# Half-unit staging of q and k, a re-woven gMLP tail, and a last unit by batch, in an attention + gMLP kernel

**Chip, cores, metric.** One core of one Trainium2 chip. The metric is device time in microseconds (us) of one execution. Each run has a state, fast or slow; ratios and comparisons here use fast runs.

## The reference

Linear attention with an exponential feature map, then a gated MLP over all heads of a position (cut to what matters):

```python
# q, k, v: (8 batches, 8 heads, 576, 64); w_phi: (64, 128)
def phi(x):
    proj = einsum('bhsd,df->bhsf', x, w_phi)
    proj = proj - max(abs(proj), axis=-1, keepdims=True)
    return concatenate([exp(proj), exp(-proj)], axis=-1)
q_p, k_p = phi(q), phi(k)
kv = einsum('bhsf,bhsd->bhfd', k_p, v); z = sum(k_p, axis=2)
x = einsum('bhsf,bhfd->bhsd', q_p, kv) / (einsum('bhsf,bhf->bhs', q_p, z) + 1e-6)   # heads joined: (8, 576, 512)
u, v = split(gelu_tanh(x @ w_in), 2)                    # w_in: (512, 1024)
v_n = (v - mean(v)) / sqrt(var(v) + 1e-6) * g_ln
out = x + (u * (w_sg @ v_n + b_sg)) @ w_out             # w_sg: (576, 576)
```

## The kernel before

The eight batches are four *units* of two batches, and a unit's attention is two *halves* of four heads. A half passes through: load of q and k (cast to 16 bit by GpSimd's DMAs, into `qks`), two merges on VectorE (`qk`), four DMA transposes (`qkT`), `nat` (projections, maxima, exponentials of k, v scaled on GpSimd), `kvsum`, `projnum`. After both halves comes the *win stage* (product with w_in, GELU, statistics, normalisation), and the *tail* (gate and output product) is woven into the two attention *stretches* of the next unit. The parts that the change touches, cuts marked `# ...`:

```python
qks = stage.tile([128, 2, H, NS, D], FP16, ...)      # a whole unit: 8 heads; the pool has one buffer
def merge(qks, h2):                                   # VectorE, into the single buffer qk
    ...
def prep(qks, h2):
    qk = merge(qks, h2)
    # ... four nc.sync.dma_start_transpose(qkT <- qk)

def norm(res):
    # ... Newton steps for 1/sqrt
    for n in range(NS):
        for pl, dst in parts:
            nc.vector.tensor_scalar(out=dst[pl, :], in0=vts[n][pl, :], ...)
            nc.gpsimd.tensor_tensor(out=dst[pl, :], in0=dst[pl, :], in1=g_bc[pl, :], op=ALU.mult)

for u in range(NU):
    if more:                                          # q and k of the next unit, all 16 loads at once
        nqk = new_qk()
        load(nc.gpsimd, u + 1, q, nqk[:, 0], both)
        load(nc.gpsimd, u + 1, k, nqk[:, 1], both)
        nT0 = prep(nqk, 0)
    # stretch 1: nat of half 1, projnum of half 0, 14 turns of the old unit's tail
    # stretch 2: nat of the next half 0, kvsum and projnum of half 1, the rest of the tail
    # ... prep(nqk, 1), win stage
weave((behind, 30, 0, 1))                             # last unit's tail
```

Program order is a wish: a scheduler orders each engine's queue by expected readiness. Line numbers in profiles belong to each kernel's own text; L91, L103 and L106 are the same merge in different kernels.

## Time and profile before

| | before |
|---|---|
| median of 3 runs | 403.94 us (402.97 to 407.26) |
| span of the profiled run, mean granted TensorE clock | 399.4 us, 0.885 |
| first bn_stats of units 0, 1, 2, 3, and end | 122.4, 200.0, 281.4, 350.6, 399.4 us |

The first bn_stats (VectorE's statistics of the v half) marks the start of a unit's win stage. The distances between these marks show which part of the kernel a gain lies in. The prediction below shows and reads the lines of the page.

### The profile page before, as it was taken

The page shows a single profiled execution, that of the slowest core. Times are in us where ns is not written, and L with a number is a line of the kernel's source. Part 1 is how long each engine was busy: PE and PEld are TensorE (multiplying, and loading weights), DVE is VectorE, ACT ScalarE, POOL GpSimd, SP SyncE. Part 2 cuts the span into 40 slices and gives each one's busy share as a digit, 9 for nine tenths or more (in the row PEclk, how much of TensorE's full clock was granted, in tenths as well). Part 3 has the DMA queues.
Part 4 walks back from the last instruction along what each step waited for, and adds up shares of the span by engine and source line. Part 5 has one row for each costly group of instructions (what it writes and reads, how often), then busy time and mean ns, then how long its engine had stood idle before and what let it go on. Part 6 is the DMA issues. An engine that isn't in the chain of part 4 may idle for free. (4 is left out here: it accounts for less than half of the span.)

```text
span 399.4 us, 7803 instructions
## 1 busy us (share of the span) xinstructions
PE 286.6 (72%) x3021; PEld 193.5 (48%) x3021; DVE 285.7 (72%) x633; ACT 245.8 (62%) x521; POOL 168.9 (42%) x189
## 2 busy tenths in 40 slices
PE   0532622866519978697898587978997879997794
PEld 0422511654405656574455465745565655544562
DVE  4549924898437999977599999756898971589530
ACT  1446113979904769478977494689767945974022
POOL 7547700567900554658208346062174550007300
PEclk9975565698858989999999699899998999999699
DMA  8988998209988200069990510544900002300015
GB/s 142 209 184 115 153 241 138 52 5 186 169 121 190 50 2 0 2 156 256 212 214 2 93 29 2 174 118 127 182 2 1 2 3 107 126 7 1 2 53 184
DMA packets 64708, 40.01 MB, mean 100 GB/s; under 512 B 35872, under 2 KB 61344, under 8 KB 64672
## 3 DMA queue, kind: packets, MB, share of 16 engines
q1 hardware_dynamic: 46128, 27.65, 29.5%
q0 software_dynamic: 18544, 11.88, 21.1%
q8 instruction: 23, 0.38, 0.4%
q14 instruction: 13, 0.11, 0.1%
HBM read 33.55 MB, written 9.44 MB: 108 GB/s over the span
## 5 line engine op out<-in xcount | busy, mean ns | idle before, releaser
L258 POOL TENSOR_TENSOR vx<-vs,vx 128x1024 f16<-128x1024 f32 (+2 forms) x48 | 71.2, 1500 | 98.8 <-ACT vx L249 89.2
L242 ACT ACTIVATE kp<-psk 128x512 f16<-128x512 f32 x144 | 81.1, 642 | 43.1 <-DVE MK L236 43.0
L316 ACT ACTIVATE qp<-pp 128x512 f16<-128x512 f32 x128 | 73.1, 657 | 10.9 <-PE pp L311 10.8
L410 POOL TENSOR_TENSOR vt<-vt,g_bc 128x512 f16<-128x512 f16 x32 | 37.7, 1207 | 80.5 <-DVE vt L408 80.2
L236 DVE TENSOR_REDUCE MK<-psk 128x4 f32<-128x512 f32 x72 | 49.1, 682 | 13.6 <-PE psk L233 13.0
L421 PE MATMUL pw<-WsgT,vt 128*128 128x288 f16 x256 | 49.6, 311 | 11.3 <-DVE uT L425 10.2
L238 DVE TENSOR_REDUCE MQ<-psq 128x4 f32<-128x512 f32 x72 | 48.9, 679 | 0.3 <-PE psq L235 0.2
L235 PE MATMUL psq<-wq,qkT 128*128 128x128 f16 x288 | 32.3, 239 | 16.9 <-DVE MQ L238 14.2
L442 ACT ACTIVATE osb<-po 128x512 f32<-128x512 f32 x36 | 22.0, 641 | 33.7 <-PE po L438 31.7
L233 PE MATMUL psk<-wk,qkT 128*128 128x128 f16 x288 | 31.8, 238 | 13.8 <-ACT qkT L217 12.2
L425 DVE TENSOR_TENSOR uT<-pw,uT 128x288 f16<-128x288 f32 x64 | 28.5, 447 | 15.9 <-PE pw L423 10.1
L421 PEld LDWEIGHTS <-vt 128*128 128x128 f16 x256 | 25.8, 105 | 25.2 <-issue 14.8
L335 PE MATMUL pn<-kvz,qp 128*128 128x65 f16 x512 | 28.5, 203 | 11.4 <-ACT qp L316 10.1
L335 PEld LDWEIGHTS <-qp 128*128 128x128 f16 x512 | 23.0, 103 | 27.5 <-ACT qp L316 23.6
L369 PE MATMUL pv<-Win,xT 128*128 128x512 f16 x144 | 35.9, 386 | 0.5 <-ACT vt L372 0.5
L382 PE MATMUL pu<-xT,Win 128*128 128x384 f16 x192 | 35.2, 325 | 0.2
L372 ACT ACTIVATE vt<-pv 128x512 f16<-128x512 f32 x36 | 21.1, 596 | 22.2 <-PE pv L369 21.9
L91 DVE COPY qk<-qks 128x2304 f16<-128x2304 f16 x16 | 13.7, 879 | 27.7 <-DMA qkT<-qk 11.8
L311 PE MATMUL pp<-qkT,wqm 66*128 66x512 f16 x72 | 29.2, 419 | 5.8 <-DMA qkT<-mT 3.3
L233 PEld LDWEIGHTS <-qkT 128*128 128x128 f16 x288 | 22.2, 107 | 20.2 <-ACT qkT L217 13.5
L235 PEld LDWEIGHTS <-qkT 128*128 128x128 f16 x288 | 22.7, 108 | 18.7 <-issue 17.8
L408 DVE TENSOR_SCALAR vt<-vt,agg,y 128x512 f16<-128x512 f16 x32 | 31.1, 1034 | 0.4
(92 smaller groups left out, 552.5 us busy)
## 6 DMA issues: line engine op xcount, KB each, us to landing
out_dram<-osb SPq DMA_DIRECT2D x32, 256.0 KB, 2.3
vs<-in_v_dram SPq DMA_DIRECT2D x16, 320.0 KB, 3.8
vs<-in_v_dram SPq DMA_DIRECT2D x16, 256.0 KB, 4.6
qks<-in_q_dram POOLq DMA_DIRECT2D x6, 320.0 KB, 10.1
qks<-in_k_dram POOLq DMA_DIRECT2D x6, 320.0 KB, 16.4
qks<-in_q_dram POOLq DMA_DIRECT2D x6, 256.0 KB, 9.0
qks<-in_k_dram POOLq DMA_DIRECT2D x6, 256.0 KB, 16.0
Win<-in_moe_w_in_dram POOLq DMA_DIRECT2D x1, 1024.0 KB, 12.7
```

Of the source, the lines that this page charges most:

```text
L233: nc.tensor.matmul(psk[:, i, :], qkT[:, n, i, :], wk[:], start=True, stop=True)
L235: nc.tensor.matmul(psq[:, i, :], qkT[:, n, i, :], wq[:], start=True, stop=True)
L236: nc.vector.tensor_reduce(out=MK[:, n, :], in_=psk[:], axis=AX.X, op=ALU.max, apply_absolute_value=True)
L238: nc.vector.tensor_reduce(out=MQ[:, n, :], in_=psq[:], axis=AX.X, op=ALU.max, apply_absolute_value=True)
L242: nc.scalar.activation(out=kp[:, e], in_=psk[:], func=AF.Exp, scale=(1.0, -1.0)[e])
L258: nc.gpsimd.tensor_tensor(out=vx[e][:, :, x0:x0 + nn, 0:64], in0=vs[:, :, n0:n1, :], in1=vx[e][:, :, x0:x0 + nn, 64:65].broadcast_to([128, ...
L316: nc.scalar.activation(out=qp[:, e], in_=pp[:], func=AF.Exp, scale=(1.0, -1.0)[e])
L335: nc.tensor.matmul(pn[:, i, :], lhs, rhs, start=(x == 0), stop=(x == len(terms) - 1))
L369: nc.tensor.matmul(pv[:], xT[:, c, n * 128:n * 128 + 128], Win[:, c, DF2:DFF], start=(c == 0), stop=(c == 3))
L382: nc.tensor.matmul(pu[:], Win[:, c, d * 128:d * 128 + 128], xT[:, c, 384 * g:384 * g + 384], start=(c == 0), stop=(c == 3))
L410: nc.gpsimd.tensor_tensor(out=dst[pl, :], in0=dst[pl, :], in1=g_bc[pl, :], op=ALU.mult)
L421: nc.tensor.matmul(pw[:], vts[5 * i + m][:, dd], WsgT[:, m, c0:c0 + 288], start=(m == 0), stop=False)
```

## The change

The intent: halve each q/k load, so that the start needs less data before it can go on, and issue a load only behind the transposes of the half before, so that the two don't cross; take g off GpSimd; spread the tail more evenly; let the last unit's gate of one batch begin before the other batch is normalised. Core of the diff:

```diff
-        return stage.tile([128, 2, H, NS, D], FP16, tag="qks", name="qks")
+    def load_qk(k, res, behind=None):
+        qks = stage.tile([128, 2, HH, NS, D], FP16, tag="qks", name="qks")   # half a unit
+        for t, src in enumerate((q, k_)):
+            for ins in load(nc.gpsimd, k // 2, src, qks[:, t], ...):
+                if behind is not None:
+                    tc.add_manual_dep(ins.ins, behind.ins.name, sync, reason="loads behind the transposes")
+                yield
-                nc.gpsimd.tensor_tensor(out=dst[pl, :], in0=dst[pl, :], in1=g_bc[pl, :], op=ALU.mult)
+                nc.vector.tensor_tensor(out=dst[pl, :], in0=dst[pl, :], in1=g_bc[pl, :], op=ALU.mult)
     def back(res):                                   # the tail
         yield from gate(res, 0)
-        # gate(res, 1) woven with wout of slots 0 to 3
+        yield from wout(res, range(0, 4))
+        yield from gate(res, 1)
         yield from wout(res, range(4, 9))
+        for k in range(NK):                          # over halves
+            qT[k + 2], last = prep(qks.pop(k + 2))
+            w.append((load_qk(k + 3, qks, last), 9, LD0, LD1))        # woven in between 0.3 and 0.8
+            # ... nat(k + 1), projnum(k)
+            w.append((behind, (12, 14)[h2], 0, 1))
+            # ... last unit:
+                weave((win_v(res, range(NS)), 10, 0, 1))
+                weave((norm(res, 0, 5, (0, 1)), 7, 0, 0.5), (win_u(res, [(0, 288), (288, 288)]), 9, 0, 1))
+                weave((gate(res, 0), 9, 0, 1), (norm(res, 5, 9, ()), 6, 0, 0.5))
+                # ... the other half of win_u, wout, gate(1), wout
```

Also: the query maxima's high and low parts (`hl`) are split from PSUM after the transpose, no longer in on-chip memory before it; w_in, g and w_out load later, and the bias row with w_sg earlier.

## The prediction

> **What bounds the kernel now.** I read the page first. No engine is full over the span, so I looked for where each stands still.
>
> ```profile
> PE 286.6 (72%) x3021; PEld 193.5 (48%) x3021; DVE 285.7 (72%) x633; ACT 245.8 (62%) x521; POOL 168.9 (42%) x189
> ...
> PEclk9975565698858989999999699899998999999699
> DMA  8988998209988200069990510544900002300015
> ```
>
> PE and DVE are equal at 72%; in the first 12 slices the DMA row is nearly full and PE's clock is low. So the kernel is two things: a start that lives on transfers, and a steady part in which PE, DVE and ACT take turns. Next I cut the span by stage in the windows view (columns: window, length, busy time of PE, PEld, DVE, ACT, POOL, PE's clock, DMA share, GB/s):
>
> ```profile
> 52.00:65.30 13.30, 2.84 (x22) 1.92 (x23) 1.53 (x3) 1.08 (x2) 0.00 (x0) 0.50 1.12 202
> ...
> 105.00:117.00 12.00, 0.71 (x10) 0.30 (x8) 0.32 (x1) 5.02 (x10) 4.61 (x5) 0.71 1.29 160
> ...
> 276.00:302.00 26.00, 23.09 (x215) 13.63 (x213) 22.44 (x50) 19.66 (x38) 12.45 (x11) 1.00 0.42 100
> ```
>
> Two windows, 25 us together, hold almost no work on any engine while the transfers are saturated. The DVE timeline names the waits in its brackets:
>
> ```profile
> 27.91 1.61 DVE L170 CAST b<-bs 128x576 f16<-128x576 f32 x1 [5.15 <-DMA bs<-in_moe_b_sg_dram]
> ...
> 38.63 4.23 DVE L276 CAST hl<-MQ 128x36 f16<-128x36 f32 x1
> ...
> 57.36 0.76 DVE L91 COPY qk<-qks 128x2304 f16<-128x2304 f16 x1 [5.34 <-DMA vs<-in_v_dram]
> 64.55 0.76 DVE L91 COPY qk<-qks 128x2304 f16<-128x2304 f16 x1 [6.44 <-DMA qks<-in_k_dram]
> ...
> 116.69 0.76 DVE L91 COPY qk<-qks 128x2304 f16<-128x2304 f16 x1 [11.76 <-DMA qkT<-qk]
> ```
>
> DVE works in order, so a merge (L91) that waits for a load holds every reduction queued behind it. Up to 65 us it waits for the whole next unit's q and k, at 105 to 117 for four DMA transposes that must empty the one qk buffer. Last, the normalisation before the gate, by its source line:
>
> ```profile
> L408 DVE TENSOR_SCALAR vt<-vt,agg,y x32: 407/1236/1303, 133.6 to 370.0; 128x512 f16<-128x512 f16 x32
> L408 DVE TENSOR_SCALAR vm<-vt,agg,y x8: 1128/1184/1234, 136.5 to 365.3; 64x512 f16<-64x512 f16 x8
> ```
>
> The triple is minimum, median and maximum in ns. An operation of 407 ns usually takes 1236, because GpSimd multiplies the preceding slot by g (L410, 1207 ns each) at the same time. In the last unit PE pays for it, as its timeline shows:
>
> ```profile
> 366.34 0.30 PE L421 MATMUL pw<-WsgT,vt 128*128 128x288 f16 x1 [0.61 <-POOL vt L410]
> 367.50 0.30 PE L423 MATMUL pw<-wsgm,vm 128*128 128x288 f16 x1 [0.86 <-POOL vm L410]
> ...
> 371.61 1.12 PE L421 MATMUL pw<-WsgT,vt 128*128 128x288 f16 x4 [3.21 <-DVE uT L425]
> ```
>
> **What the Trainium skill says.** (1) SBUF — State Buffer, section Who interferes with whom: GpSimd and a DVE instruction in a 2-port mode share a port pair, and whoever issues second blocks until the first is done; tensor_scalar can be such an instruction. The trace agrees: 407 against 1236 ns. The hl cast (L276) has a median of 169 ns and takes 4232 ns once, at 38.6 us, while GpSimd works. (2) VectorE: DVE Perf Modes, section The perf-mode tier table: a 16-bit tensor_tensor reaches 2x, 1224 ns at 2048 elements, hence an estimate of (256+151)/0.96 = 424 ns at 512. No such operation runs on DVE before, so the trace cannot say. (3) DMA: Bandwidth & Descriptors, section Issuing engines are not separate DMA queues: all queues share the 16 DMA engines. The trace agrees: a transpose lands after 3.4 us at best and 14.4 at worst, the worst beside a q/k load. (4) TensorE: Matmul & The Clock Gate, section What's actually happening: an idle PE falls to half clock. The 0.50 in the window above agrees.
>
> **The change part by part.** From the order view of both kernels as built.
>
> *Staging by half unit.* The bytes stay the same. Each load is now half as large, and is issued only when the transposes of the half before have landed. Before the second half's reductions can start, DVE now needs three halves of q and k rather than four. One half is 8 loads of 128 to 160 KB on the way in, 2.36 MB of float32 (4 heads x 2 batches x 576 x 64 x 4 bytes x 2 tensors). Unit 1's 4.7 MB plus v's 1.2 MB took from 42.8 to 64.5 us, about 270 MB per ms, so one half is 8.7 us. The saving is about one half less the new dependency (transposes alone take some 6 us, at 66 to 72): I take 6 us, so the reductions start near 58 instead of 65. The bias load also comes ahead of half of v, which removes most of the 5.15 us wait; and hl is now made from PSUM, which cannot be locked out for 4.2 us. These two lie before 52 us and are mostly covered by the same transfers, so I add nothing for them. After that, transposes and loads no longer overlap: the 11.76 us wait at 105 falls away, as the next load is issued behind the transposes and lands well inside a stretch of about 25 us (6 + 8.7 + 8 issues of 0.7 us). I leave 1 us for a shorter wait of the third half's merge. Sum to the start of the first win stage (first bn_stats at 122.4 us): 6 + 11.8 - 1 = 17 us earlier, near 105.
>
> *g on DVE.* Per unit GpSimd loses 10 operations of 1.2 us. DVE gains 10 of 0.42, and its 10 tensor_scalars fall from 1.2 to 0.41. Together 10 x (0.41 + 0.42) = 8.3 us, less about 0.1 each where neighbours overlap (a 0.68 us reduction starts 0.60 after its neighbour), so 7 us. Before it lasted from 291.85 to 302.0, 10.2 us. The gate ends its first product on DVE just after; PE has finished win_u by 297.7 and then does little. So 3 us come off in each of three win stages, and about 1 more as PE no longer runs the next few us at half clock (PEclk 0.93 in 302 to 326, which is 3.4 us at half speed, 1.7 lost). 4 x 3 = 12 us.
>
> *Tail over two stretches.* 12 of 25 pieces go into the first stretch and 13 into the second, now one kind after another. Before it was 14, then 11 over 18 places, so the second stretch ran out of them and ended on ACT alone (9.97 of 10 us busy at 190 to 200, PE 8.4). Work does not fall. With hl free of the lock (L276 and L277 took 13.2 us where 16 operations at 0.18 would take 3), I give 0.7 us for each of six stretches: 4 us.
>
> *Last unit by batch.* Before, first batch's gate reached its full pace at 371.6. Now only 5 slots need normalising first: the last slot's statistics at 358.5, the Newton steps partly woven in, 5 slots x 0.75 = 3.5, so near 363. PE has half of win_u until 361. Then gate 8 x 0.77 = 6.2, win_u 4, four wout 4 x 1.08, gate 6.2, five wout 5.4 = 26 us, with about 1 of waits: 390 against 395.5 for the last product. 6 us. Everything sums to 17 + 12 + 4 + 6 = 39, and 403.9 - 39 = 365.
>
> **The rivals.** *The chain load, merge, transpose, load becomes the bound.* It is serial by construction: about 6 + 2 + 5.6 + 8.7 = 22 us per half, with 3 to 4 more if v or the output runs beside it. Against a stretch of 25 that is tight, and a single staging buffer gives no slack. For it: seven halves, and DMA shares over 1.2 in the first 60 us. Against it: every second stretch is followed by a win stage of 24 us that needs no q or k. If it holds in three stretches at 4 us each, the time is 377. *DVE becomes the bound* through 40 added multiplications, if the tensor_tensor is at 1x: (512+151)/0.96 = 691 ns, 2.7 us more per unit, so the win stages gain 1 instead of 4: 374. Against it: all operands are 16 bit and dense. *The start is bounded by bytes anyway*: w_in, w_out and w_sg (4.3 MB) also move in the first 60 us, and the order view has them before the second half's transposes end. Then the first 6 us go, 371. *Better than thought*: with DVE free of locks PE could near 90% in the stretches, 2 us more in each: 353.
>
> **Range and chances.** The stall of 11.8 us and the locks are in plain sight and the change removes their causes, so a gain over 2% (8 us) is nearly sure: 0.96; within 2% 0.03; slower 0.01. The rivals give 353 to 377; not all at once, so 354 to 380 should hold 8 in 10, the upper side longer as two of them could add up.
>
> **What would show it.** Right: no stretch of 10 us in which all engines idle after 70 us; first bn_stats at 100 to 110; vt tensor_scalar's median near 410 ns and its multiplication near 424; the last matmul of the span some 47 us after the last unit's first bn_stats drops to about 41; GpSimd busy about 47 us less. Wrong: a merge with a bracket of 4 us or more on a q/k load in the later stretches; a tensor_tensor of 690 ns; a first bn_stats after 115. The prediction as a whole fails if units still take 76 us between their first bn_stats.

## The result

385.5 us (median of 4; 383.46, 384.31, 386.70 fast, 391.28 slow), against 403.78 beside it. The ratio, which is the mean of one kernel's fast runs over that of the other's of the same rounds and so not quite the ratio of the medians, is 0.9515, interval 0.943 to 0.960. Faster, by half of what I predicted, and outside the range. Ratios of later runs are made in the same way.

First two parts of the changed kernel's page, the lines that answer to those of before:

```profile
PE 291.3 (76%) x3037; PEld 199.5 (52%) x3037; DVE 265.0 (69%) x680; ACT 246.3 (65%) x525; POOL 137.0 (36%) x173
...
PEclk9998585886589998999999899989999998799999
DMA  7996997288599705591992059902500020210024
```

GpSimd lost 32 us of work and VectorE 21, and PE's share rose by 4 points in a span that is 18 us shorter. I had forecast 47 for GpSimd: the products by g are gone, but q and k are now loaded in 64 pieces instead of 40, and issuing them takes 41.6 us of its queue instead of 27.2. PE's clock still has two dips between slices 20 and 30 (the 8s, at 210 to 219 and 248 to 258 us), where the start is long over; in the kernel before there are a 6 and an 8. Marks of both profiled runs:

| | first bn_stats, unit 0 | unit 0 to 1 | 1 to 2 | 2 to 3 | last unit to end |
|---|---|---|---|---|---|
| before | 122.4 | 77.6 | 81.4 | 69.2 | 48.8 |
| changed | 113.2 | 74.2 | 82.0 | 66.3 | 46.0 |

The start gave 9.2 of 17 us; the unit from 1 to 2 gave nothing. The normalisation did as predicted. Its two operations by source line (minimum/median/maximum in ns, then first and last start in us):

```profile
L425 DVE TENSOR_SCALAR vt<-vt,agg,y x32: 394/408/415, 123.5 to 353.1; 128x512 f16<-128x512 f16 x32
L427 DVE TENSOR_TENSOR vt<-vt,g_bc x32: 411/419/423, 124.2 to 353.8; 128x512 f16<-128x512 f16 x32
```

The first was 1236 at the median; the second is the 424 of the estimate. The "wrong" sign is there too. VectorE's timeline of the changed kernel (start, duration, instruction, in brackets the idle time before it and what ended it), at three merges:

```profile
58.05 0.76 DVE L103 COPY qk<-qks 128x2304 f16<-128x2304 f16 x1 [7.67 <-DMA qks<-in_q_dram]
61.02 0.76 DVE L103 COPY qk<-qks 128x2304 f16<-128x2304 f16 x1 [2.20 <-DMA qks<-in_k_dram]
61.81 0.69 DVE L252 TENSOR_REDUCE MK<-psk 128x4 f32<-128x512 f32 x1
...
236.03 0.76 DVE L103 COPY qk<-qks 128x2304 f16<-128x2304 f16 x1 [4.41 <-DMA qks<-in_k_dram]
```

In all, merges waited 31.0 us for loads, 7.2 of them for the very first half. Why they waited at 236 is in GpSimd's timeline of the changed kernel:

```profile
218.40 1.94 POOL L274 TENSOR_TENSOR vx<-vs,vx 128x1024 f16<-128x1024 f32 x1 [29.43 <-ACT vx L265]
...
222.86 1.30 POOL L77 DMA_DIRECT2D qks<-in_q_dram  x2
...
227.59 0.61 POOL L272 TENSOR_TENSOR vx<-vs,vx 128x256 f16<-128x256 f32 x1
228.16 1.05 POOL L274 TENSOR_TENSOR vx<-vs,vx 128x512 f16<-128x512 f32 x1
229.16 2.67 POOL L77 DMA_DIRECT2D qks<-in_k_dram  x4
```

The four q loads had been issued by 225.4. The k loads stood in the queue behind the v multiplications (`vx`), which themselves wait for ScalarE's exponentials, and were issued at 229.2 only. The Trainium skill, "TensorE: Matmul & The Clock Gate", section Architectural detail: the array is 16× 32×32, not 1× 128×128, says that VectorE's queue is strictly first in, first out, and GpSimd's too, on each of its cores. The trace agrees: the k loads start at 229.16, right behind the product that starts at 228.16 and takes 1.05.

The start shows a second cost of the staging, which I had overlooked. GpSimd's timelines, the loads of half 1, first of the kernel before, then of the changed kernel:

```profile
6.70 1.31 POOL L73 DMA_DIRECT2D qks<-in_q_dram  x2
```

```profile
17.04 2.48 POOL L77 DMA_DIRECT2D qks<-in_q_dram  x4 [4.73 <-DVE qk L103]
```

With one buffer of half a unit, half 1's loads wait until half 0 is merged, and start 10 us later than before. Half 2's loads start at 48.3, behind the transposes; before, the whole next unit's start at 39.1.

### The profile page after: what moved, and what is told of

Same layout as the page of the kernel before. It is cut to its first block, busy times and chain, and to the rows that moved or that the text cites. A ratio compares the mean times of both kernels' runs of the same rounds, so it can differ in the third digit from the quotient of the medians.

```text
span 381.7 us, 7907 instructions
## 1 busy us (share of the span) xinstructions
PE 291.3 (76%) x3037; PEld 199.5 (52%) x3037; DVE 265.0 (69%) x680; ACT 246.3 (65%) x525; POOL 137.0 (36%) x173
## 4 chain that ended last, share of the span: by engine, by line
PE 29%; ACT 20%; DMA 14%; DVE 13%; POOL 12%; issue 9%; SPq 1%; ACTq 0%; DVEq 0%; POOLq 0%
DMA qks<-in_k_dram 8%; ACT qp L329 7%; ACT kp L258 7%; PE pu L399 5%; POOL qks L77 5%; POOL vx L274 5%; PE pw L439 4%; PE pv L383 4%; PE po L456 3%; PE pkv L313 2%; PE pn L348 2%; DVE bst L388 2%; DMA qkT<-qk 2%; DVE MK L252 2%; DMA wn<-in_moe_w_sg_dram 2%
## 5 line engine op out<-in xcount | busy, mean ns | idle before, releaser
L439 PE MATMUL pw<-WsgT,vt 128*128 128x288 f16 x256 | 45.8, 293 | 5.3 <-DVE uT L443 5.1
L249 PE MATMUL psk<-wk,qkT 128*128 128x128 f16 x288 | 33.8, 241 | 15.4 <-ACT qkT L232 9.6
L443 DVE TENSOR_TENSOR uT<-pw,uT 128x288 f16<-128x288 f32 x64 | 28.6, 450 | 18.3 <-PE pw L441 16.5
L348 PE MATMUL pn<-kvz,qp 128*128 128x65 f16 x512 | 29.5, 205 | 13.8 <-ACT qp L329 11.5
L401 ACT ACTIVATE uT<-pu 128x384 f16<-128x384 f32 (+1 forms) x52 | 24.3, 466 | 19.2 <-PE pu L399 18.4
L103 DVE COPY qk<-qks 128x2304 f16<-128x2304 f16 x16 | 14.6, 918 | 31.6 <-DMA qks<-in_k_dram 16.3
L460 ACT ACTIVATE osb<-po 128x512 f32<-128x512 f32 x36 | 24.2, 681 | 18.6 <-PE po L456 14.2
L399 PE MATMUL pu<-xT,Win 128*128 128x384 f16 (+1 forms) x208 | 35.6, 312 | 0.3 <-ACT vt L386 0.2
L383 PE MATMUL pv<-Win,xT 128*128 128x512 f16 x144 | 34.0, 384 | 1.2 <-ACT vt L386 1.1
L249 PEld LDWEIGHTS <-qkT 128*128 128x128 f16 x288 | 22.9, 108 | 22.6 <-ACT qkT L232 11.2
L439 PEld LDWEIGHTS <-vt 128*128 128x128 f16 x256 | 24.5, 99 | 18.6 <-issue 10.4
L251 PEld LDWEIGHTS <-qkT 128*128 128x128 f16 x288 | 23.5, 110 | 18.7 <-issue 17.4
L313 PE MATMUL pkv<-vx,kp 128*128 128x65 f16 x512 | 28.8, 208 | 5.0 <-POOL vx L274 5.0
L456 PE MATMUL po<-Wout,uT 128*128 128x512 f16 x108 | 31.5, 386 | 0.0
```

What stands on the lines that cost most here:

```text
L249: nc.tensor.matmul(psk[:, i, :], qkT[:, n, i, :], wk[:], start=True, stop=True)
L251: nc.tensor.matmul(psq[:, i, :], qkT[:, n, i, :], wq[:], start=True, stop=True)
L348: nc.tensor.matmul(pn[:, i, :], lhs, rhs, start=(x == 0), stop=(x == len(terms) - 1))
L383: nc.tensor.matmul(pv[:], xT[:, c, n * 128:n * 128 + 128], Win[:, c, DF2:DFF], start=(c == 0), stop=(c == 3))
L399: nc.tensor.matmul(pu[:, 0:w], Win[:, c, d * 128:d * 128 + 128], xT[:, c, t0:t0 + w], start=(c == 0), stop=(c == 3))
L439: nc.tensor.matmul(pw[:], vts[5 * i + m][:, dd], WsgT[:, m, c0:c0 + 288], start=(m == 0), stop=False)
```

## Experiments

All runs gave correct results. Runs with the same number in the last column ran on the same chip, one after the other, and share the runs of the kernel before. Each has six runs; the highest of e2, e7, e14 and e15 is a slow one. First bn_stats, waits and tails are read from one profiled run each, all fast.

| run | edit | median us (lowest to highest) | ratio to before (interval) | call |
|---|---|---|---|---|
| e1_loads_first | changed, q/k loads ahead of `vx` | 375.52 (372.30 to 376.61) | 0.9298 (0.926 to 0.934) | 1 |
| e2_bias_late | changed, bias copies late | 386.95 (384.38 to 390.43) | 0.9588 (0.953 to 0.964) | 1 |
| e3_g_on_gpsimd | changed, g back on GpSimd | 404.42 (402.54 to 407.05) | 1.0039 (0.999 to 1.009) | 1 |
| e4_end_old | changed, old order of the last unit | 386.71 (386.12 to 388.92) | 0.9609 (0.957 to 0.965) | 1 |
| e5_merge_later | e1, first merge behind reductions | 370.39 (368.88 to 371.03) | 0.9154 (0.911 to 0.920) | 2 |
| e6_before_g_vector | before, g on VectorE | 384.05 (383.77 to 387.41) | 0.9525 (0.947 to 0.958) | 2 |
| e7_weave_old | changed, old weave | 383.27 (380.07 to 387.16) | 0.9466 (0.941 to 0.952) | 2 |
| e8_not_behind | e1, no dependency on transposes | 374.20 (370.70 to 376.21) | 0.9243 (0.919 to 0.930) | 2 |
| e9_old_end | e5, old order of the last unit | 367.52 (366.90 to 368.90) | 0.9099 (0.906 to 0.914) | 3 |
| e10_old_weave | e9, old weave | 372.28 (371.82 to 372.84) | 0.9214 (0.917 to 0.926) | 3 |
| e11_bias_in_gap | e9, bias copies in a gap | 367.74 (366.40 to 369.61) | 0.9108 (0.906 to 0.916) | 3 |
| e12_old_hl | e9, old `hl` | 368.87 (366.49 to 371.03) | 0.9130 (0.908 to 0.918) | 3 |
| e13_staged_by_unit | before, g + new weave + new `hl` | 385.78 (384.08 to 389.45) | 0.9557 (0.951 to 0.961) | 4 |
| e14_not_behind | e9, no dependency on transposes | 369.23 (366.13 to 371.83) | 0.9120 (0.907 to 0.917) | 4 |
| e15_two_stages | e14, two buffers for `qks` | 363.09 (360.22 to 366.19) | 0.8967 (0.892 to 0.901) | 4 |
| e16_norm_longer | e6, each g product done twice | 404.23 (400.63 to 405.14) | 1.0003 (0.995 to 1.005) | 5 |

### Where the staging's gain went

My theory after the traces: the place of the k loads in GpSimd's queue. The main rival: the waits are the serial chain through one buffer, wherever the loads stand.

```diff
-                    w.append((load_qk(k + 3, qks, last), 9, LD0, LD1))
+                    for _ in load_qk(k + 3, qks, last):
+                        pass
+    # and an order-only dependency: the first vx product of nat(k + 1) after those loads
```

> Changed kernel with one edit: the eight q/k loads of half k+3 are issued on GpSimd before the v multiplications of half k+1 instead of among and behind them. Queue-order theory: the vector engine's waits for q/k at the merges (16.3 + 14.7 us in the changed kernel's trace, of which about 13 us lie from 81 us on) fall below 4 us, the units come 2 to 3 us closer together and the time is 376 to 380. Rival (serial chain of load, merge, transposes: the wait is the chain itself, not its place in the queue): the merges still wait as long, time within 1 us of the changed kernel. Rival (the waits are slack, another engine ends the stretch): the waits go but the first bn_stats of each unit stays where it is, time within 2 us of 385.

Measured: 375.5, 8.8 us better by the ratios (0.0217 x 404). GpSimd's timeline of this run, at the same place:

```profile
204.95 1.26 POOL L79 DMA_DIRECT2D qks<-in_q_dram  x2
206.16 2.50 POOL L79 DMA_DIRECT2D qks<-in_k_dram  x4
216.03 3.82 POOL L277 TENSOR_TENSOR vx<-vs,vx 128x1024 f16<-128x1024 f32 x2 [7.36 <-ACT vx L268]
```

The merges that follow, at 225.28 and 226.83, have no bracket. The unit from 1 to 2 takes 74.4 us, not 82.0. So the queue theory holds for the steady part; at the start the merges still wait (18.3 us in all: 7.1 for the very first half and 11.1 at 59 and 62 us), so my "below 4 us" failed, and the first bn_stats is even later, at 116.8.

For the start I first suspected set-up work, 22 copies made from the bias row, which the change put ahead of the first reductions.

```diff
         bs = work.tile([128, S], F32, tag="uT", name="bs")
+        nc.vector.tensor_copy(out=bs[:, 0:1], in_=MQs[0][:, 35:36])   # holds the load back
```

> Changed kernel with the bias row's load and the 22 vector copies made from it held back behind the last reduction of the first half, as they were in the kernel before. Theory that the start lost its gain to set-up work moved ahead of the first half: merges of half 0 back to about 10 and 13 us, first reduction at about 16 us instead of 21.4, first bn_stats of unit 0 at 107 to 109 instead of 113.2, time 379 to 382. Rival (the second half's loads end at the same time anyway, because its loads and w_sg wait behind each other): first reduction earlier but merge of half 1 and 2 and first bn_stats unchanged, time within 1 us of the changed kernel. Third: the copies only move into the second half, where the vector engine is busy, and take 3 us back.

Measured: the first reductions came at 16.8 instead of 21.4 and half 1's at 58.2 instead of 61.8, but the copies then took some 7 us of VectorE between 78 and 86 us, as the third theory said, and the first bn_stats stayed at 112.5. A second try put them into a gap in which VectorE waits anyway:

```diff
-        nc.vector.tensor_copy(out=bh, in_=bs[:])
+        c = nc.vector.tensor_copy(out=bh, in_=bs[:])
+        tc.add_manual_dep(c.ins, red[0, 8].ins.name, order, reason="after the first half")
```

> e9_old_end with the 22 vector copies of the bias row behind the last reduction of the first half, into the gap of some 9 us in which the vector engine waits for transposes and half 2's loads; the load of the row stays where it is. If these copies are on the path of the start: first reduction at about 17 us instead of 21.4, first bn_stats of unit 0 earlier by 3 to 4.5, time shorter by as much. If the start is bound by the bytes loaded up to half 1 and 2 (all q/k merges find their data at the same time as before): no difference over 1 us. A third: the copies do not fit the gap and put off the first reduction of half 1 (50.5 us).

Measured: 367.74 against e9's 367.52, first bn_stats 110.5 against 110.4. These copies are not on the path; this suspicion falls.

In the lines of the result VectorE was free from 50.4 us; half 1's reductions stood behind two merges of half 2, which waited for loads.

```diff
-                qT[k + 2], last = prep(qks.pop(k + 2))
+                qT[k + 2], last = prep(qks.pop(k + 2), red[1, 3] if k == 0 else None)
+    # prep and the loads of half 3 are woven in at 0.35 of the first stretch, the merges after reduction red[1, 3]
```

> The kernel with the loads first (e1_loads_first, 375.5) with one more edit: in the first stretch the two merges of half 2 stand behind the fourth group of reductions of half 1 on the vector engine, instead of ahead of all of them. Theory (the second half's reductions start at 62 us and not at about 49 because merges that wait 8.9 us for half 2's loads stand ahead of them in the in-order queue): first reduction of half 1 at 48 to 52 us, wait at the merge under 4 us, first bn_stats of unit 0 at 107 to 111 instead of 116.8, time 366 to 370. Rival (half 2's loads, merge, transposes and reductions are the chain that ends the second stretch, so the start comes from bytes): reductions of half 1 start earlier but the first bn_stats stays within 2 us of 116.8 and the time within 2 us of 375.5.

Measured: 370.4; first reduction at 50.5, first bn_stats at 110.2 instead of 116.8. VectorE's timeline of this run, where the changed kernel stood still:

```profile
50.53 0.69 DVE L257 TENSOR_REDUCE MK<-psk 128x4 f32<-128x512 f32 x1
...
58.58 0.76 DVE L106 COPY qk<-qks 128x2304 f16<-128x2304 f16 x1 [0.65 <-DMA qks<-in_q_dram]
...
61.53 0.76 DVE L106 COPY qk<-qks 128x2304 f16<-128x2304 f16 x1 [1.39 <-DMA qks<-in_k_dram]
```

The loads land when they did; the order of the queue is what changed. Next, what holds the loads: the dependency behind the transposes, or the single buffer.

```diff
-                    for _ in load_qk(k + 3, qks, last):
+                    for _ in load_qk(k + 3, qks):
```

> The kernel with the loads first (375.5) without the dependency that holds the q/k loads behind the last transposes: they then wait only for the merges to free the single staging buffer. If the dependency does what the change's title says (keeps the loads from crossing the transposes, which slows these and what waits on them): transposes take longer, 377 to 385. Rival (it only delays the loads by some 10 us): merges find their data earlier, 370 to 374. Third: neither shows, within 1.5 us of 375.5.

> e9_old_end (367.5) without the dependency that puts the q/k loads behind the transposes; one staging buffer still. From e8_not_behind (374.2 against 375.5): 365 to 367, the merges of half 3 (78.2 and 84.5 us) some 5 us earlier. If the loads then cross the transposes and slow them: 368 to 371.

Measured: 374.2 against 375.5 and 369.2 against 367.5, with overlapping intervals both times, once shorter and once longer. So the dependency does nothing to the time that I can measure. It moves the waits: without it the first bn_stats comes earlier (108.6 against 116.8, 108.3 against 110.4) and the next unit takes as much longer (77.3 against 71.2, 76.6 against 71.0), and in e14 a merge of half 3 waits 7.0 us for transposes at 80 us, where in e9 it waits 4.7 for loads at 78.

```diff
-        qks = stage.tile([128, 2, HH, NS, D], FP16, tag="qks", name="qks")
+        qks = stage.tile([128, 2, HH, NS, D], FP16, tag="qks", name="qks", bufs=2)
```

> e14_not_behind with two staging buffers for q/k, so that a half's loads wait for neither the merge nor the transposes of the half before. Serial-chain theory of the start (load, merge, next load through one buffer sets the first bn_stats): merges of half 2 and 3 have their data, waits there under 2 us, first bn_stats of unit 0 at 104 to 107, time 361 to 365. Byte-bound start: merges wait about as long as in e14_not_behind, first bn_stats within 1.5 us, time within 1 us of it.

Measured: 363.1, first bn_stats at 100.5 instead of 108.3. The merges of this run by source line and what they waited for in all (us, times):

```profile
L106 DVE COPY qk<-qks x16: 726/773/1579, 10.6 to 214.2; 128x2304 f16<-128x2304 f16 x16
its engine sat idle before it (us, times) until:
  DMA qkT<-qk: 4.5, 1
  DMA qks<-in_k_dram: 2.3, 1
  DMA qks<-in_q_dram: 2.2, 1
```

Half 1's loads go out early again, as GpSimd's timeline of this run shows, and half 1's merges come at 27.5 us instead of 34.8:

```profile
6.70 1.31 POOL L79 DMA_DIRECT2D qks<-in_q_dram  x2
```

So the serial chain that the prediction named as a rival was real in the first 100 us, but as a matter of one buffer, not of bytes: the bytes are the same. One thing is not separated: the scheduler also moved the w_sg load (from 6.7 to 28.4 us) and the bias copies (from 16.6 to 31.6 us) behind these loads. With one buffer, moving the copies alone gained nothing (e11). The two waits on loads that are left are those of the very first half. The wait of 4.5 us on the transposes that read the merged buffer (`qk`) is left too; a version with a second `qk` doesn't build (8 KB per partition needed for the last pool, 3.03 left). This is the fastest version, 10% below before.

Is the half-unit staging itself worth anything? The kernel before with all but the staging and the last unit's order:

```diff
-                nc.gpsimd.tensor_tensor(out=dst[pl, :], in0=dst[pl, :], in1=g_bc[pl, :], op=ALU.mult)
+                nc.vector.tensor_tensor(out=dst[pl, :], in0=dst[pl, :], in1=g_bc[pl, :], op=ALU.mult)
+    # and back(), the normalisation woven with win_u, the shares 12 and 14, and hl as in the changed kernel
```

> Kernel before (q/k staged by whole unit, loads issued a unit ahead) with three parts of the change: g on the vector engine, the new weave of the tail, the query maxima split out of PSUM; the last unit in the old order. All but the staging by half unit. If the staging itself is worth what its start shows (first bn_stats 113.2 against 122.4): 380 to 383, first bn_stats at 122 to 124, the later units as close together as in e9_old_end (71 to 74.5 us). If the staging costs as much later as it gives at the start, once its loads are well placed: 367 to 372. If the staged loads are what the new weave needs: 383 to 386, no better than e6_before_g_vector (384.0).

Measured: 385.8, the third outcome. Against e9_old_end, which has the same parts and the staging with its queues in order, the staging is worth 0.0458 x 404 = 18.5 us, of which 13.8 lie before the first bn_stats (124.2 against 110.4). With the old weave on both sides (e10, with the new `hl`, against e6, with the old one) it is 0.0311 x 404 = 12.6. Both differences hold the new places of the loads of w_in, g, w_out and w_sg too, which no run separates.

### What g is worth

> Changed kernel with the multiplication by g back on GpSimd, as in the kernel before. My prediction's step (g on VectorE is worth 4 us in each of 3 win stages, 12 in all): 394 to 398. Rival, that it is worth what the win stages' measured difference says (21.2 to 18.6, 20.4 to 21.2, 20.5 to 18.8, so about 2 each at most): 388 to 391, with normalisations of 10 us again. Third: GpSimd's longer queue also delays the q/k loads that stand behind it, so it costs more than the 12.

```diff
-                nc.vector.tensor_tensor(out=dst[pl, :], in0=dst[pl, :], in1=g_bc[pl, :], op=ALU.mult)
+                nc.gpsimd.tensor_tensor(out=dst[pl, :], in0=dst[pl, :], in1=g_bc[pl, :], op=ALU.mult)
```

Measured: 404.4, the whole gain gone, which fits the third alone. And alone, on the kernel before:

```diff
-                nc.gpsimd.tensor_tensor(out=dst[pl, :], in0=dst[pl, :], in1=g_bc[pl, :], op=ALU.mult)
+                nc.vector.tensor_tensor(out=dst[pl, :], in0=dst[pl, :], in1=g_bc[pl, :], op=ALU.mult)
```

> Kernel before with one edit: g multiplied on the vector engine. Prediction's step: 12 us of the change's 18 come from this alone, so 391. Reading of e3_g_on_gpsimd (taking it back costs 19 in the changed kernel) under theory A, that g alone is the whole gain and the staging with the new weave gives nothing: 384 to 387. Theory B, that the two depend on each other (g's 34 multiplications in GpSimd's queue hold back the staged loads, which the kernel before issues a whole unit ahead, and share the vector engine's port): 391 to 397.

Measured: 384.05, 0.0475 x 404 = 19 us, theory A. One line gives what the whole change gave; the rest of the change as built adds up to nothing. The four win stages are shorter by 12.3 us (marks to the first gate product: 21.2, 20.4, 20.5, 20.5 us before; 18.3, 17.4, 17.4, 17.2 here). The two profiled runs lie 17.4 us apart; the rest is some 6 us in the stages after the win stages (the start is 1.1 later). The windows view around unit 0's first gate products, first of the kernel before, then of e6 (columns: window, length, busy time of PE, PEld, DVE, ACT, POOL, PE's granted clock, DMA share, GB/s):

```profile
139.00:142.00 3.00, 2.80 (x24) 1.79 (x23) 3.00 (x3) 2.28 (x4) 2.85 (x3) 1.00 0.00 0
142.00:144.00 2.00, 0.00 (x0) 0.00 (x0) 2.00 (x4) 0.98 (x2) 2.00 (x3) 1.00 0.00 0
144.00:147.00 3.00, 2.55 (x17) 1.70 (x17) 2.69 (x6) 2.30 (x5) 1.82 (x2) 0.53 0.01 3
147.00:150.00 3.00, 3.00 (x39) 2.51 (x37) 2.43 (x7) 2.06 (x5) 0.00 (x0) 0.90 0.02 5
```

```profile
142.00:144.00 2.00, 1.78 (x18) 1.27 (x16) 1.89 (x5) 1.99 (x3) 0.00 (x0) 1.00 0.00 0
144.00:147.00 3.00, 3.00 (x43) 2.35 (x41) 3.00 (x9) 3.00 (x8) 0.00 (x0) 1.00 0.01 3
```

In the kernel before, TensorE has its first two gate products ready, VectorE is still normalising and cannot take them, and TensorE stands for 2.3 us; then it runs at half clock for about 3 us. In e6 its longest stand here is 0.2 us, and its clock stays full. Is it the pause, or GpSimd working beside VectorE? A normalisation of the old length without GpSimd:

```diff
+                nc.vector.tensor_tensor(out=junk[pl, :], in0=dst[pl, :], in1=g_bc[pl, :], op=ALU.mult)
                 nc.vector.tensor_tensor(out=dst[pl, :], in0=dst[pl, :], in1=g_bc[pl, :], op=ALU.mult)
```

> e6_before_g_vector (384.0) with each multiplication by g done twice on the vector engine, once into a scratch tile: the normalisation lasts about 4 us longer (10 x 0.42), as long as with GpSimd in the kernel before, but GpSimd does nothing in it. Theory that the 20 us are the normalisation's length (about 3 us in each of 4 win stages) and the clock that TensorE loses in the pause (7 us in the stages after, clock 0.885 against 0.918): 400 to 404, clock near 0.885. If the clock has nothing to do with the pause: 396 to 398, clock near 0.918. If GpSimd's running beside the vector engine is what costs: 384 to 390, as some of the longer normalisation hides.

Measured: 404.2, ratio 1.000, clock of its fast runs 0.878 to 0.893 against 0.903 to 0.923 in e6. TensorE's lines at the pause, first of the kernel before, then of this run, and this run's windows:

```profile
144.12 0.87 PE L421 MATMUL pw<-WsgT,vt 128*128 128x288 f16 x3 [2.33 <-DVE uT L425]
```

```profile
146.19 0.65 PE L423 MATMUL pw<-WsgT,vt 128*128 128x288 f16 x4 [1.96 <-DVE uT L427]
```

```profile
144.00:146.00 2.00, 0.23 (x2) 0.00 (x0) 2.00 (x7) 1.89 (x4) 0.00 (x0) 1.00 0.00 0
146.00:149.00 3.00, 2.04 (x22) 1.67 (x22) 3.00 (x9) 1.56 (x3) 0.00 (x0) 0.68 0.00 0
149.00:152.00 3.00, 3.00 (x28) 2.33 (x27) 2.84 (x8) 2.08 (x5) 0.00 (x0) 0.50 0.02 5
```

So 40 more products of 0.42 us on VectorE (its busy time rises by 12.2 us, as they overlap their neighbours) cost 19 (0.0478 x 404), as much as GpSimd's part had cost, with GpSimd idle beside them. The two cases don't match in every part: the normalisation lasts 11.4 to 12.1 us here and 10.1 in the kernel before, and the first gate product comes ahead of its end. Up to that product the four win stages take 83.3 us here, 82.6 before and 70.4 in e6. So about 12 of the 19 lie in the win stages both times, and some 6 in the stages after. From 125 us on TensorE's mean clock is 0.96 before, 0.94 here and 1.00 in e6. That the lower clock makes up those 6 us is likely, but not shown: from 301.9 to 326 us the kernel before has a clock of 0.93, and takes no longer than e6 for the same work (24.1 us). The port lock that I read from the 1236 ns is real; a cost beyond the length that it gives the normalisation doesn't show in these runs.

### The weave, hl and the last unit

The old weave, in the changed kernel (e7) and in e9 (e10):

```diff
         yield from gate(res, 0)
-        yield from wout(res, range(0, 4))
-        yield from gate(res, 1)
+        first, second = gate(res, 1), wout(res, range(0, 4))
+        # ... four times: two turns of first, one of second
         yield from wout(res, range(4, 9))
-                w.append((behind, (12, 14)[h2], 0, 1))
+                w.append((behind, (14, 18)[h2], 0, 1))
```

> Changed kernel with the old order of the gMLP tail: gate 1 woven with the first output products, shares of 14 and 18 turns in the two stretches. Prediction's step (new weave and hl from PSUM are worth 0.7 us in each of 6 stretches, 4 together): 387 to 390. Rival (the new weave gives nothing): within 1.5 us of 385.5.

> e9_old_end with the old order of the gMLP tail in the two stretches too (gate 1 woven with the first output products, 14 and 18 turns). Prediction's step (new weave is most of 0.7 us in each of 6 stretches): 3 to 4 us longer than e9_old_end. Reading of e7_weave_old (383.3 against 385.5): within 2 us of e9_old_end, either way.

Measured: in the changed kernel the old weave is, if anything, better (383.3 against 385.5, intervals overlapping); with the queues in order the new weave is 4.8 us better (372.3 against 367.5, ranges apart). What was predicted is there, but shows only in this kernel: with whole-unit staging, the new weave and `hl` gain nothing either (e13 against e6). Why is not shown.

```diff
-        nc.tensor.transpose(pm[:], MQf[:], ident32[:])
-        nc.vector.tensor_copy(out=hl[0:36, 0, :], in_=pm[0:36, :])
-        nc.vector.tensor_tensor(out=hl[0:36, 1, :], in0=pm[0:36, :], in1=hl[0:36, 0, :], op=ALU.subtract)
+        nc.vector.tensor_copy(out=hl[:, 0, :], in_=mqf)
+        nc.vector.tensor_tensor(out=hl[:, 1, :], in0=mqf, in1=hl[:, 0, :], op=ALU.subtract)
+        nc.tensor.transpose(pm[0:72, :], hl.rearrange("p t x -> p (t x)"), ident[:])
+        nc.vector.tensor_copy(out=mT[0:72, :], in_=pm[0:72, :])
```

> e9_old_end with the query maxima split into two halves in on-chip memory before the transpose, as in the kernel before (two vector casts of about 0.97 us and one copy in the place of two of about 0.28 us, eight times). If on the path: about 1 us in each of 7 halves, 5 to 8 us longer. Prediction's step (most of 0.7 us a stretch is the new weave, hl a part): 1 to 3 us longer. Rival: hidden, within 1 us.

Measured: 1.3 us longer than e9, ranges overlapping: at most small.

The last unit in its old order, in the changed kernel (e4) and in e5 (e9):

```diff
-                # the seven weaves by batch
+                # win_v of all slots, win_u of a third, norm of all slots, win_u of the rest
+                weave((win_old(), 22, 0, 1))
+                # gate 0, then gate 1 woven with wout of slots 0 to 3, then wout of slots 4 to 8
+                weave((back_old(), 30, 0, 1))
```

> Changed kernel with the last unit's gMLP in the order of the kernel before (all of the v and u halves, one normalisation, then both gates woven with the first output product). Prediction's step (by batch is worth 6 us): 391 to 392. Rival (the second batch's normalisation sits inside the first gate, and the end is bound by TensorE at whatever order): 384 to 388; end from first bn_stats 46 to 49 us.

> The kernel with loads first and the first merge later (e5_merge_later, 370.4) with the last unit's gMLP in the order of the kernel before. Prediction's step (by batch is worth 6): 376. Reading of the two tails (45.9 us from the last unit's first bn_stats to the end in e5_merge_later, 43.4 in the kernel before with g on the vector engine): 367.5 to 369.5, tail 43 to 44. Rival from e4_end_old (386.7 against 385.5 for the changed kernel): 370 to 372.

Measured: on the changed kernel no clear difference; on e5 the old order takes 367.5 against 370.4, with intervals that just overlap. The tails agree both times: 44.2 us in e4 against 46.0, 43.8 in e9 against 45.9. TensorE's timeline of e5, the two gate products that waited longest:

```profile
336.27 0.65 PE L446 MATMUL pw<-WsgT,vt 128*128 128x288 f16 x4 [0.57 <-DVE uT L450]
341.47 0.65 PE L446 MATMUL pw<-WsgT,vt 128*128 128x288 f16 x4 [2.42 <-DVE uT L450]
```

The second batch's normalisation sits in VectorE's queue among the products of the first gate, and TensorE waits 2.4 us for it; cutting the u half into 64 matmuls of 288 columns instead of 48 of 384 costs 0.8 us more (9.4 against 8.6 busy).

## Why the prediction was wrong

- **Start, 17 us: failed, 9.2 in the changed kernel.** The step that failed is "the reductions start near 58 instead of 65": they started at 61.8. I counted bytes; but half 1's loads went out 10 us later than before, half 2's 9 us later than the next unit's had, and two merges of half 2 stood ahead of half 1's reductions. Moving those merges took the first bn_stats from e1's 116.8 to 110.2. The 11.76 us wait did fall away as said, but "I leave 1 us for a shorter wait of the third half's merge" was far too little: half 2's merges waited 9.9 us, half 3's 4.8. With two staging buffers, which the prediction did not have, the start came 7.8 us earlier than in e14, to 100.5.
- **"The next load ... lands well inside a stretch of about 25 us": failed.** I added durations and didn't ask where the loads stand in GpSimd's queue. They stood behind the v multiplications, which cost 8.8 us. This is a wait that took the place of the one removed: the kernel before issues a whole unit's loads together, and its merges waited for none of them after 65 us. The halved loads also cost twice the issues per byte.
- **g, 3 x 4 = 12 us: right mechanism, too small.** Measured 19. The direct 3 us hold in each stage, but there are four stages (I put the last under the next step), and the stages after them gave some 6 where I had 3 for the clock.
- **Tail and hl, 4 us: right in size (4.8, and up to 1.3) with the queues in order, but not there in the kernel as built** (e7).
- **Last unit by batch, 6 us: failed.** Its tail became 2.8 us shorter than before, but g alone does 5.4 (48.8 to 43.4); the order itself costs about 2. I had compared it with a kernel in which GpSimd still held the gate. I also took 395.5 us for the end of the last product; the trace has 394.8.
- **Rival "serial chain": it named the right danger** but had it as time that doesn't fit into a stretch, 4 us in three stretches. What the runs show is two queue orders and one buffer, together 8.8 + 5.8 (e1 to e5, by ratios) + 6.2 (e14 to e15).
- **Smaller readings.** The window of 105 to 117 us was not empty: ScalarE worked 5.0 us of it and GpSimd 4.6. w_in, w_out and w_sg are 4.5 MB, not 4.3. Neither carries the sum.

In sum, by ratios and in this order: g 19, the staging and weave with queues in order about 17 (e6 to e9), given back in the kernel as built by the place of the loads (8.8), of the merges (5.8) and by the last unit's order (2.2). The place of the loads weighs most: mended alone, it gave 375.5 (e1).

Left open: why e1 by itself made the first bn_stats 3.6 us later than in the changed kernel; how much of g's 19 us is the clock; why the new weave gains in one kernel only; and whether the same two-buffer edit would do as much without the edits to the queues.

## What to carry to other kernels

When a transfer is made smaller or later, find its issue in the queue of the engine that issues it, and its first consumer in that engine's queue: a load behind work that waits for another engine, or a waiting copy ahead of ready work, takes the gain back. Half the size is twice the issues, and a smaller buffer must be emptied before the next load can start. Measure each part of a change alone on the kernel before; here one line was worth all of it and the rest only after mending. Look at what follows a pause of TensorE too: here the half clock came after some pauses of about 2 us and not after others.

## What the Trainium skill lacked or had wrong

- "TensorE: Matmul & The Clock Gate", section What's actually happening: the pause that costs the clock is given as about 3.4 us. Here a pause of 2.3 us (before, ahead of 144.12 us) and one of 2.0 us (e16, ahead of 146.19) were followed by the half clock for some 3 and nearly 7 us, in e16 only 0.9 us after the pause. Other pauses of 2.0 us, ahead of 169.17 us in the kernel before and of 167.29 in e6, were followed by full clock. So the length of a pause alone doesn't tell. Ends of matmuls are modelled in the trace, so the pauses are uncertain by a few tenths.
- "SBUF — State Buffer", section Who interferes with whom: right on the lock (407 against 1236 ns). It doesn't say what a lock costs on the path; here a normalisation lengthened on VectorE alone gave the same total (404.2 against 403.3 us).
- "VectorE: DVE Perf Modes", section The perf-mode tier table: right. The estimate of 424 ns worked out from its figure measured 419.
- "DMA: Bandwidth & Descriptors", section Anatomy of one DMA — SWDGE (gpsimd) path: it calls descriptor generation small and puts most of a transfer's fixed cost on its completion. Here the issue of eight q/k loads took 5.2 us of GpSimd's queue (0.65 each), and their place among its other work was worth 8.8 us; I found no page that warns of this.
